# A two-layer expert network behind clustered attention: batch 1's tiles spaced wider, four tiles of batch 0 transposed on TensorE, sums of |v| on ScalarE

## The chip, the cores and the metric

One Trainium2 chip, one core of it. The metric is the device time in microseconds of one execution, lower is better; the median of three runs is given. TensorE is called PE in the rows, VectorE DVE, ScalarE ACT, GpSimd POOL and SyncE SP.

## The reference

Two batches of eight heads of attention with 768 queries and keys of width 64. A key is only seen by queries of the same cluster, where the cluster is the nearest of 16 centroids per head. The 1536 x 512 result then goes through two expert layers, each of two matrix products (512 to 2048 and back).

```
q_assign = argmax(q_n @ c_n.T); k_assign = argmax(k_n @ c_n.T)      # per head, normalised
scores = where(q_assign == k_assign, q @ k.T / 8, -1e9)
attn = softmax(scores); x = (attn @ v)  ->  [1536, 512]
h = x @ w_in;  g = max(h, 0) + alpha * min(h, 0);  x = g @ w_out       # layer 1
h = x @ w_in2; g = h * clip(h + 3, 0, 6) / 6;      out = g @ w_out2    # layer 2
```

Inputs and output are float32; the products are made of a high and a low part each, so that a product of two matrices is three passes on TensorE. The weights stand in memory as 64-bit values and are turned into float32 in the kernel.

## The kernel before

The kernel records operations and does not write them down in order: `op(engine, cost, fn, r, w, acq, vt, ...)` keeps an operation with what it reads and writes, the buffers it takes, an estimated cost and a due time `vt`. `Planner.plan` then walks through time: each engine that is free takes the ready operation with the smallest due time for which buffers are free, for as long as its cost says. The start times of that plan are the order in which the instructions are issued, on every engine's own in-order queue. So the numbers at the top (`U0`, `T1`, `DU`, `T2`, `PREP0`, `ST`, ...) and the costs set the order and nothing else.

*Attention* (`attention`) runs for batch 0 and then for batch 1, as four pairs of heads (`prep`) of twelve tiles each (`head`, 128 queries by 768 keys; 48 tiles a batch). `prep` transposes q and k of a pair on TensorE (L461), splits them into high and low parts, makes the logits of the clusters (L518) from `cs`, which GpSimd fills from the centroid blocks `ccol` (L505, L507), picks the cluster on VectorE (L531 to L566), and scales v by a power of two taken from the maximum of |v| (L590 to L627). A tile makes its scores on TensorE (L662, a PSUM buffer `ps`), their minimum on VectorE (L669), the exponential on ScalarE (L696 or L676), and a high and a low part of 16 bits (`hl`, L730 and L734, or L681 and L685). These are transposed by a DMA on SP's queue into `pt` (`turn`, L640), and 18 short matmuls with v end the tile (`pv`, L647). Some tiles of batch 0 (`t % 4 == 2`) are transposed on TensorE instead (L709), with the two parts made behind it (L714, L718). From `EARLY = 44` on, the last four tiles of batch 0 take the way of L676, L681, L685 and the DMA. The due time of tile u is `U0 * u` in batch 0 and `T1 + 5 + DU * u` in batch 1.

*The expert layers* (`moe`) follow for batch 0 with due times from T1 to T1 + T2, and at the same time the tiles of batch 1 are worked off; then for batch 1 alone. A product is 12 matmuls: of w_in (`g_in`, L894, then ScalarE L902 or L911, VectorE L906 or L915) or w_out (`g_out`, L943 in layer 1, L946 in layer 2). L915 belongs to layer 2 alone. For batch 0 each of the 64 weight tiles (`weight`) is loaded (L800, L803), converted on ScalarE (L809) and VectorE (L814, L821, L827), stored for batch 1 (L832), and split by ScalarE and GpSimd (L836, L841). For batch 1 it is loaded back (L792).

## Time and profile before

| | |
|---|---|
| median of 3 runs | 828.1 us (825.6 to 828.75) |
| profiled execution | 828.88 us |
| its span, first to last instruction | 826.8 us |
| busy: TensorE, VectorE, ScalarE, GpSimd | 752.8, 522.7, 472.1, 477.9 us |
| mean granted TensorE clock | 0.959 |

The profile is of one execution. Busy times are sums over the span and hide that the stretches differ: the attention of batch 0, batch 0's expert layers with the attention of batch 1, and batch 1's expert layers have different busiest engines.

### The profile page before, as it was taken

The page shows a single profiled execution, that of the slowest core. Times are in us where ns is not written, and L with a number is a line of the kernel's source. Part 1 is how long each engine was busy: PE and PEld are TensorE (multiplying, and loading weights), DVE is VectorE, ACT ScalarE, POOL GpSimd, SP SyncE. Part 2 cuts the span into 40 slices and gives each one's busy share as a digit, 9 for nine tenths or more (in the row PEclk, how much of TensorE's full clock was granted, in tenths as well). Part 3 has the DMA queues.
Part 4 walks back from the last instruction along what each step waited for, and adds up shares of the span by engine and source line. Part 5 has one row for each costly group of instructions (what it writes and reads, how often), then busy time and mean ns, then how long its engine had stood idle before and what let it go on. Part 6 is the DMA issues. An engine that isn't in the chain of part 4 may idle for free.

```text
span 826.8 us, 14279 instructions
## 1 busy us (share of the span) xinstructions
PE 752.8 (91%) x5331; PEld 696.7 (84%) x5331; DVE 522.7 (63%) x882; ACT 472.1 (57%) x768; POOL 477.9 (58%) x450
## 2 busy tenths in 40 slices
PE   5667877678999999989999999999999999999997
PEld 4556766668999888879899988789999999899986
DVE  7997888988879988988986788621122222122222
ACT  6777858766576676676666554544433254443421
POOL 3685685638553574654765565765566377464630
PEclk9988898859999999998999999999999999999999
DMA  6589989998699999599985564543222121221201
GB/s 131 119 170 227 176 151 198 168 238 210 182 209 201 203 221 229 117 222 208 213 226 187 177 191 156 191 117 111 64 77 64 45 84 52 64 76 53 76 10 68
DMA packets 214533, 121.56 MB, mean 147 GB/s; under 512 B 171072, under 2 KB 191552, under 8 KB 214464
## 3 DMA queue, kind: packets, MB, share of 16 engines
q1 hardware_dynamic: 214464, 120.66, 61.4%
q8 instruction: 41, 0.67, 0.4%
q14 instruction: 28, 0.23, 0.1%
HBM read 61.38 MB, written 21.50 MB: 100 GB/s over the span
## 4 chain that ended last, share of the span: by engine, by line
PE 58%; DVE 17%; DMA 10%; ACT 6%; issue 4%; POOL 3%; SPq 1%; POOLq 0%; ACTq 0%; DVEq 0%
PE pb L894 12%; PE pc L894 12%; PE pc L943 7%; PE pb L943 6%; PE pc L946 6%; PE pb L946 5%; DMA pt<-hl 4%; PE ps L662 4%; DVE wf L821 3%; DVE junk L669 3%; PE ps L518 3%; DVE wf L827 3%; DMA wd<-in_moe_w_in_dram 2%; DVE wf L814 1%; PE pb L647 1%
## 5 line engine op out<-in xcount | busy, mean ns | idle before, releaser
L841 POOL TENSOR_TENSOR w<-wf,w 128x512 fp32r<-128x512 f32 x128 | 167.5, 1312 | 171.1 <-ACT w L836 122.9
L924 POOL TENSOR_TENSOR big<-t,big 128x384 fp32r<-128x384 f32 x128 | 139.0, 1090 | 80.9 <-ACT big L920 74.3
L894 PE MATMUL pb<-xh,w 128*128 128x384 f32 x528 | 143.5, 338 | 1.7 <-DVE vs L613 1.7
L894 PE MATMUL pc<-xh,w 128*128 128x384 f32 x496 | 136.7, 341 | 0.0
L836 ACT CAST w<-wf 128x512 fp32r<-128x512 f32 x125 | 77.0, 618 | 83.7 <-DVE wf L827 37.7
L734 POOL TENSOR_TENSOR hl<-e,hl 128x768 f16<-128x768 f32 x53 | 90.3, 1711 | 47.4 <-ACT hl L730 38.6
L894 PEld LDWEIGHTS pb<-xh,w 128*128 128x128 f32 x528 | 96.5, 187 | 2.4 <-DVE vs L613 2.0
L669 DVE TENSOR_SCALAR_CACHE_REDUCE junk<-ps 128x768 bf16<-128x768 f32 x96 | 91.0, 948 | 10.4 <-PE ps L662 7.6
L894 PEld LDWEIGHTS pc<-xh,w 128*128 128x128 f32 x496 | 91.6, 189 | 0.2
L894 PE MATMUL pb<-xl,w 128*128 128x384 f32 x264 | 89.1, 338 | 0.0
L920 ACT CAST big<-t 128x384 fp32r<-128x384 f32 x124 | 63.2, 513 | 41.1 <-DVE t L915 20.0
L894 PE MATMUL pc<-xl,w 128*128 128x384 f32 x248 | 84.2, 340 | 0.0
L946 PE MATMUL pc<-w,big 128*128 128x512 f32 x312 | 77.0, 400 | 2.0 <-POOL big L924 1.9
L662 PE MATMUL ps<-big,big 128*128 128x384 f32 x192 | 59.6, 394 | 18.9 <-ACT e L696 6.2
L943 PE MATMUL pb<-big,w 128*128 128x384 f32 x396 | 75.8, 344 | 0.3 <-ACT t L999 0.3
L946 PEld LDWEIGHTS pc<-w,big 128*128 128x128 f32 x312 | 59.2, 192 | 16.2 <-POOL big L924 3.6
L943 PE MATMUL pc<-big,w 128*128 128x384 f32 x372 | 71.5, 342 | 0.0
L943 PEld LDWEIGHTS pb<-big,w 128*128 128x128 f32 x396 | 70.9, 190 | 0.6 <-ACT t L999 0.4
L696 ACT ACTIVATE e<-ps,mn 128x768 f32<-128x768 f32 x60 | 53.6, 902 | 23.6 <-DVE junk L669 22.1
L821 DVE SCALAR_TENSOR_TENSOR wf<-wd,wf 128x512 int32<-128x512 int32 x64 | 66.0, 1031 | 1.3
L943 PEld LDWEIGHTS pc<-big,w 128*128 128x128 f32 x372 | 66.3, 190 | 0.0
L946 PE MATMUL pb<-w,big 128*128 128x512 f32 x264 | 63.9, 393 | 2.0 <-POOL big L924 2.0
(144 smaller groups left out, 1335.5 us busy)
## 6 DMA issues: line engine op xcount, KB each, us to landing
wd<-in_moe_w_in_dram SPq DMA_DIRECT2D x32, 512.0 KB, 4.5
w<-wf SPq DMA_DIRECT2D x64, 256.0 KB, 3.2
wd<-in_moe_w_out_dram SPq DMA_DIRECT2D x32, 512.0 KB, 4.3
wf<-w SPq DMA_DIRECT2D x64, 256.0 KB, 2.6
raw_q<-in_q_dram SPq DMA_DIRECT2D x16, 192.0 KB, 3.7
raw_k<-in_k_dram SPq DMA_DIRECT2D x16, 192.0 KB, 3.8
raw_v<-in_v_dram SPq DMA_DIRECT2D x16, 192.0 KB, 3.3
out_dram<-acc SPq DMA_DIRECT2D x12, 256.0 KB, 2.0
```

Of the source, the lines that this page charges most:

```text
L662: nc.tensor.matmul(ps.ap[:, kk, 0:NH], s[x].ap[:, i, c0:c0 + 128], s[y].ap[:, kk, :], start=(n == 0), stop=(n == 1))
L669: nc.vector.tensor_scalar(out=junk.rearrange("p (a b) -> p a b", a=2), in0=ps.ap[:, :, 0:NH], scalar1=LN_P, scalar2=None, op0=ALU.add, op1 ...
L696: nc.scalar.activation(out=e.ap.rearrange("p (a b) -> p a b", a=2), in_=ps.ap[:, :, 0:NH], func=ACTF.Exp, bias=mn.ap, scale=-1.0)
L734: tt_on(eng)(out=hl.ap[:, 1, :], in0=e.ap, in1=hl.ap[:, 0, :], op=ALU.subtract)
L821: nc.vector.scalar_tensor_tensor(out=wi, in0=wd.ap[:, :, 1], scalar=-0x80000000, in1=wi, op0=ALU.bitwise_and, op1=ALU.bitwise_or)
L836: copy_on(e)(w.ap[:, 0, :], wf.ap)
L841: tt_on(e)(out=w.ap[:, 1, :], in0=wf.ap, in1=f32(w.ap[:, 0, :]), op=ALU.subtract)
L894: nc.tensor.matmul(hp.ap[:, 0:NH], w.ap[:, hw, 128 * kk:128 * kk + 128], (xl if hx else xh)[i][:, kk, :], start=(m == 0), stop=(m == 3 * K ...
L920: copy_on(e)(g.ap[:, 0, :], t.ap)
L924: tt_on(e)(out=g.ap[:, 1, :], in0=t.ap, in1=f32(g.ap[:, 0, :]), op=ALU.subtract)
L943: nc.tensor.matmul(o.ap[:, 0:NH], w.ap[:, hw, 128 * e:128 * e + 128], g.ap[:, hg, :], start=(m == 0), stop=(m == 3 * FC - 1))
L946: nc.tensor.matmul(o.ap, g.ap[:, hg, 128 * e:128 * e + 128], w.ap[:, hw, :], start=(m == 0), stop=(m == 3 * FC - 1))
```

## The change

The table of numbers at the top changes, and with it the order. Batch 1's tiles are due every 5.216 instead of every 3.672, so that they reach further into the expert layers of batch 0, which in turn are due within 313 instead of 329. Some twelve estimated costs change too. In the code, the last four tiles of batch 0 are transposed on TensorE (L709 before), as every fourth was. The scale of v is taken from the sum of |v| over each partition's 384 values times 2^-9, made by two ScalarE activations with an accumulator, and no longer from a maximum on VectorE. The centroid blocks `ccol` and the memset of `cs` go from VectorE to GpSimd. A one-column exponential is issued right behind the square root, so that its table is loaded there.

```diff
-U0, PREP0, SPAN0 = 2.2, -23.969, 15.768
-T1, DU, PREP1, SPAN1 = 110.562, 3.672, -22.219, 20.627
-T2, LEAD, LOADS = 329.488, 19.217, 14.435
-S_AT, PV_AT, LAZY = -0.999, -0.056, 0.0
+U0, PREP0, SPAN0 = 2.345, -16.443, 11.495
+T1, DU, PREP1, SPAN1 = 110.896, 5.216, -24.195, 27.638
+T2, LEAD, LOADS = 313.132, 24.352, 12.015
+S_AT, PV_AT, LAZY = -3.092, 1.619, 0.0
...
+        op("ACT", 1.5, lambda: nc.scalar.activation(out=first, in_=three, func=ACTF.Exp), r=["three"], w=["first"],
+           after=[o], vt=vt)
...
-            nc.vector.tensor_scalar(out=ccol[:, 0, :], in0=f32(hi), scalar1=-1.0, scalar2=None, op0=ALU.mult)
...
+            nc.gpsimd.tensor_scalar(out=ccol[:, 0, :], in0=f32(hi), scalar1=-1.0, scalar2=None, op0=ALU.mult)
...
-                nc.vector.tensor_reduce(out=va.ap[:, 0, :], in_=vr.ap, axis=AX.XY,
-                                        op=ALU.max, apply_absolute_value=True)
-            op("DVE", 0.87, f, r=[(vr, 0), (vr, 1)], w=[(va, 0)], acq=[va], vt=vt)
+                for j in range(2):
+                    nc.scalar.activation(out=junk2.rearrange("p (t d) -> p t d", t=NT), in_=vr.ap[:, j], func=ACTF.Abs,
+                                         scale=2.0 ** -9, accum_out=va.ap[:, 0, j:j + 1])
+            op("ACT", 1.1, f, r=[(vr, 0), (vr, 1)], w=[(va, 0)], acq=[va], vt=vt)
...
-                if late and (b == 0 or t % 3):
+                if b and t % 3:
...
-                if b == 0 and t % 4 == 2:
+                if b == 0 and (late or t % 4 == 2):
```

What the order does at two places. First VectorE's queue around the last tiles of batch 0, before (`wf` are weight tiles, `hl` low parts of tiles, `xl` the attention result's low part for the expert layers):

```order
L685 SCALAR_TENSOR_TENSOR hl_118<-ps_154,hl_118 128x768
L814 TENSOR_SCALAR wf_97<-wf_97 128x512
L602 TENSOR_REDUCE va_135<-pb_158 2x1
L603 TENSOR_SCALAR va_135<-va_135 2x1
L605 TENSOR_SCALAR va_135<-va_135 2x1
L607 TENSOR_SCALAR va_135<-ident,va_135 2x2
L993 SCALAR_TENSOR_TENSOR xl_74<-pb_157,xh_72 128x384
```

And after, where L727 is the low part behind a transpose on TensorE, L830 and L836 are the weights' (L821, L827 before), L1002 is L993 before, and L680 the minimum:

```order
L727 SCALAR_TENSOR_TENSOR acc_106<-ps_156,acc_106 128x768
L823 TENSOR_SCALAR wf_96<-wf_96 128x512
L830 SCALAR_TENSOR_TENSOR wf_96<-wd_94,wf_96 128x512
L727 SCALAR_TENSOR_TENSOR acc_105<-ps_157,acc_105 128x768
L836 SCALAR_TENSOR_TENSOR wf_96<-wd_94,wf_96 128x512
L823 TENSOR_SCALAR wf_97<-wf_97 128x512
L755 TENSOR_SCALAR sm_150<-pb_159,vs_135 128x6
L757 RECIPROCAL sm_150<-sm_150 128x6
L758 TENSOR_TENSOR xn_137<-pb_159,sm_150 128x6x64
L830 SCALAR_TENSOR_TENSOR wf_97<-wd_95,wf_97 128x512
L680 TENSOR_SCALAR junk,mn_141<-ps_155 128x768
L836 SCALAR_TENSOR_TENSOR wf_97<-wd_95,wf_97 128x512
L1002 SCALAR_TENSOR_TENSOR xl_74<-pb_159,xh_72 128x384
```

The first product's L906 is row 248 of VectorE's order before; after, it is row 231 (as L915 there). Next SP's queue in the second expert layer of batch 0, before (L803 and L800 load weights, L832 stores them, L1000 is the last pair's result of batch 1's attention):

```order
L832 DMA w_159<-wf_96 128x512
L1000 DMA xb<-t_101 128x384
L1000 DMA xb<-t_102 128x384
L803 DMA wd_94<-in_moe_w_out_dram 128x1024
L832 DMA w_159<-wf_97 128x512
L803 DMA wd_95<-in_moe_w_out_dram 128x1024
```

And after, likewise at two loads of w_out (L812 and L809 load, L841 stores, L651 is the transposing DMA of a tile):

```order
L841 DMA w_160<-wf_96 128x512
L812 DMA wd_94<-in_moe_w_out_dram 128x1024
L651 DMA_TRANSPOSE pt_109<-hl_118 128x12x128
L651 DMA_TRANSPOSE pt_108<-hl_119 128x12x128
L812 DMA wd_95<-in_moe_w_out_dram 128x1024
L841 DMA w_160<-wf_97 128x512
```

Before, the last pair of batch 1 is through when these loads stand there; after, its tiles still stand between loads.

## Rows read from the trace of the kernel before

**Rows 1.** The page: busy us of the engines (share of the span, instructions), and shares of the span in the chain that ended last, by engine.

```profile
PE 752.8 (91%) x5331; PEld 696.7 (84%) x5331; DVE 522.7 (63%) x882; ACT 472.1 (57%) x768; POOL 477.9 (58%) x450
...
PE 58%; DVE 17%; DMA 10%; ACT 6%; issue 4%; POOL 3%; SPq 1%; POOLq 0%; ACTq 0%; DVEq 0%
```

**Rows 2.** Single instructions in order of time on TensorE and VectorE: start and duration in us, engine, line, operation.

```profile
180.33 0.67 PE L894 MATMUL pc<-xh,w 128*128 128x384 f32 x1
...
395.41 0.34 PE L894 MATMUL pc<-xh,w 128*128 128x384 f32 x1
...
397.53 0.34 PE L894 MATMUL pb<-xh,w 128*128 128x384 f32 x1
...
401.52 0.69 DVE L827 SCALAR_TENSOR_TENSOR wf<-wd,wf 128x512 uint32<-128x512 uint32 x1
402.12 0.95 DVE L685 SCALAR_TENSOR_TENSOR hl<-ps,hl 128x768 f16<-128x768 f32 x1
...
403.94 0.54 DVE L915 SCALAR_TENSOR_TENSOR t<-t,pc 128x384 f32<-128x384 f32 x1
```

**Rows 3.** Pieces of the chain that ended last, in order of time: start and length in us, engine, tile, line, matmuls.

```profile
144.67 3.21 PE pb L647 x90
...
271.79 0.65 PE ps L461 x6
...
283.57 1.48 PE ps L662 x8
...
542.57 4.19 PE pc L894 x24
...
703.09 5.50 PE pb L946 x24
```

**Rows 4.** Busy time of each engine in four stretches: from and to, length in us, busy us (instructions) of PE, PE's weight loads, DVE, ACT, POOL, then the granted clock, the DMA engines' busy share and GB/s.

```profile
0.00:180.33 180.33, 127.81 (x1327) 109.19 (x1328) 153.66 (x300) 131.79 (x170) 109.70 (x130) 0.86 0.88 173
180.33:395.41 215.08, 202.84 (x1702) 193.68 (x1701) 189.54 (x315) 144.40 (x233) 121.86 (x109) 0.97 0.89 202
395.41:542.57 147.16, 143.65 (x830) 130.15 (x830) 113.70 (x159) 82.75 (x149) 92.29 (x75) 0.99 0.67 192
542.57:826.80 284.23, 278.55 (x1476) 263.67 (x1475) 65.75 (x110) 113.16 (x216) 154.02 (x138) 1.00 0.22 66
```

**Rows 5.** VectorE's groups of instructions by line: operation, tiles, shapes, count, busy us and mean ns of one, idle us ahead of them and who ended it.

```profile
L669 DVE TENSOR_SCALAR_CACHE_REDUCE junk<-ps 128x768 bf16<-128x768 f32 x96 | 91.0, 948 | 10.4 <-PE ps L662 7.6 <-DVE junk L669 0.5 <-PE pb L597 0.2
L821 DVE SCALAR_TENSOR_TENSOR wf<-wd,wf 128x512 int32<-128x512 int32 x64 | 66.0, 1031 | 1.3
L827 DVE SCALAR_TENSOR_TENSOR wf<-wd,wf 128x512 uint32<-128x512 uint32 x64 | 59.3, 927 | 0.8
L814 DVE TENSOR_SCALAR wf<-wf 128x512 int32<-128x512 int32 x64 | 41.9, 655 | 16.1 <-ACT wf L809 16.1
L685 DVE SCALAR_TENSOR_TENSOR hl<-ps,hl 128x768 f16<-128x768 f32 x36 | 34.1, 949 | 4.2 <-ACT hl L681 1.9 <-POOL v L627 1.4 <-DMA w<-wf 0.6
...
L491 DVE SCALAR_TENSOR_TENSOR kb<-ps,big 64x768 fp32r<-64x768 f32 x16 | 15.2, 953 | 0.4 <-ACT big L487 0.2
...
L543 DVE TENSOR_TENSOR eq<-lg,mx 128x384 bf16<-128x384 f32 x8 | 9.6, 1197 | 0.1
L531 DVE STREAM_TRANSPOSE lg<-ps 128x384 f32<-128x384 f32 x16 | 8.5, 562 | 7.4 <-PE ps L518 7.0 <-ACT kb L575 0.3
L566 DVE STREAM_TRANSPOSE lg<-oh 128x768 f32<-128x768 f32 x8 | 7.8, 971 | 3.8 <-POOL oh L561 3.8
L669 DVE DVE_READ_ACCUMULATOR junk<-ps 128x1 f32 x96 | 7.7, 80 | 0.0
L590 DVE TENSOR_REDUCE va<-raw_v 128x2 f32<-128x768 f32 x8 | 7.6, 952 | 0.6 <-DMA raw_v<-in_v_dram 0.3
...
L556 DVE TENSOR_TENSOR eq<-desc,mx 128x384 bf16<-128x384 bf16 x8 | 5.2, 650 | 0.1
...
L535 DVE TENSOR_REDUCE mx<-lg 128x24 f32<-128x384 f32 x8 | 4.3, 541 | 0.0
...
L718 DVE SCALAR_TENSOR_TENSOR acc<-ps,acc 128x768 f16<-128x768 f32 x4 | 3.8, 944 | 0.7 <-ACT acc L714 0.7
...
L358 DVE MEMSET cs<- 128x1024 f32 x1 | 0.9, 912 | 0.2 <-issue 0.2
...
L410 DVE CAST ccol<-chi 64x128 fp32r<-64x128 f32 x2 | 0.5, 236 | 0.0
```

**Rows 6.** The same columns as rows 4, for the stretch up to the first instruction of layer 2 on VectorE.

```profile
0.00:403.94 403.94, 337.93 (x3081) 309.65 (x3082) 351.60 (x627) 282.24 (x413) 237.27 (x243) 0.92 0.89 189
```

**Rows 7.** Two of ScalarE's groups by line, with the columns of rows 5.

```profile
L911 ACT ACTIVATE t<-pb,three 128x384 f32<-128x384 f32 x34 | 19.7, 579 | 22.5 <-PE pb L894 22.5
...
L990 ACT CAST xh<-pb 128x384 fp32r<-128x384 f32 x8 | 3.8, 477 | 3.8 <-PE pb L761 3.7
```

**Rows 8.** ScalarE's instructions around the first exponential, in order of time; in brackets the idle time ahead of one, and who ended it.

```profile
27.64 1.28 ACT L696 ACT_TABLE_LOAD   x1
29.13 0.90 ACT L696 ACTIVATE e<-ps,mn 128x768 f32<-128x768 f32 x1 [0.21 <-DVE junk L669]
```

**Rows 9.** DMA issues by line: queue, operation, count, median us from issue to landing.

```profile
pt<-hl SPq DMA_TRANSPOSE x69, 4.7
```

**Rows 10.** Waits of SP's queue: us in total, times, longest us; the first from 180.33 to 395.41 us, the second from 395.41 to 542.57.

```profile
SPq L640 <- DVE hl L685: 28.6, 13, 7.3
...
SPq L803 <- DVE wf L827: 20.9, 5, 4.7
```

More of the change, by code (lines that the diff above doesn't have):

```diff
@@ L313 @@
     junk = sb.tile([128, S], BF16, name="junk")
+    junk2 = sb.tile([128, NT * D], BF16, name="junk2")
     hls = slots(2, [128, 2, S], FP16, "hl")
@@ L346, in constants @@
         cn = sm.tile([128, 2, D], F32, name="cn")
+        first = sm.tile([128, 1], F32, name="first")
         hi = sm.tile([128, 128], F32R, name="chi")
@@ L357, in f @@
             nc.vector.memset(f32(ccol), 0.0)
-            nc.vector.memset(f32(cs), 0.0)
-        op("DVE", 2.0, f, w=["cs", "three", "ones", "ccol"], vt=vt)
+        op("DVE", 1.1, f, w=["three", "ones", "ccol"], vt=vt)
         def f():
@@ L370, in constants @@
         op("POOL", 3.6, f, w=["desc", "oh", "kb", "v1"], vt=vt)
+        op("POOL", 1.0, lambda: nc.gpsimd.memset(f32(cs), 0.0), w=["cs"], vt=20.0)
         def f():
@@ L383, in constants @@
         op("DVE", 0.4, f, r=["cr"], w=["ss"], vt=vt)
-        op("ACT", 0.1, lambda: nc.scalar.activation(out=ss[:, 1:2], in_=ss[:, 0:1], func=ACTF.Sqrt), w=["ss"], vt=vt)
+        o = op("ACT", 0.1, lambda: nc.scalar.activation(out=ss[:, 1:2], in_=ss[:, 0:1], func=ACTF.Sqrt), w=["ss"], vt=vt)
+        op("ACT", 1.5, lambda: nc.scalar.activation(out=first, in_=three, func=ACTF.Exp), r=["three"], w=["first"],
+           after=[o], vt=vt)
         def f():
@@ L404, in f @@
                                            op0=ALU.mult, op1=ALU.subtract)
-            nc.vector.tensor_scalar(out=ccol[:, 0, :], in0=f32(hi), scalar1=-1.0, scalar2=None, op0=ALU.mult)
-            nc.vector.tensor_scalar(out=ccol[:, 1, :], in0=f32(lo), scalar1=-1.0, scalar2=None, op0=ALU.mult)
+        op("DVE", 0.6, f, r=[pt], w=["chl"], vt=vt)
+        def f():
+            nc.gpsimd.tensor_scalar(out=ccol[:, 0, :], in0=f32(hi), scalar1=-1.0, scalar2=None, op0=ALU.mult)
+            nc.gpsimd.tensor_scalar(out=ccol[:, 1, :], in0=f32(lo), scalar1=-1.0, scalar2=None, op0=ALU.mult)
             for j in range(2):
                 a, z = slice(64 * j, 64 * j + 64), slice(64 - 64 * j, 128 - 64 * j)
-                nc.vector.tensor_copy(ccol[a, 2 + 2 * j, :], f32(hi)[a])
-                nc.vector.tensor_copy(ccol[z, 2 + 2 * j, :], f32(lo)[z])
-                nc.vector.tensor_copy(ccol[a, 3 + 2 * j, :], f32(hi)[a])
-        op("DVE", 1.6, f, r=[pt], w=["ccol"], vt=vt)
+                nc.gpsimd.tensor_copy(ccol[a, 2 + 2 * j, :], f32(hi)[a])
+                nc.gpsimd.tensor_copy(ccol[z, 2 + 2 * j, :], f32(lo)[z])
+                nc.gpsimd.tensor_copy(ccol[a, 3 + 2 * j, :], f32(hi)[a])
+        op("POOL", 2.0, f, r=["chl"], w=["ccol"], vt=vt)
         op("SP", 0.5, lambda: nc.sync.dma_start(out=alpha_sb, in_=moe_alpha.rearrange("(k p) -> p k", p=128)),
@@ L520, in prep @@
                               (("qa", "h"), ("qa", "l"), ("ka", "h"), ("ka", "h2"), ("kb", "l"))]
-                op("PE", 1.3, f, r=r + [(s["kb"], "m") for s in st], w=[(pl, i)],
+                op("PE", 1.42, f, r=r + [(s["kb"], "m") for s in st], w=[(pl, i)],
                    acq=[pl] if i == 0 else [], vt=vt, lat=0.3)
@@ L544, in f @@
                                         op=ALU.is_equal)
-            op("DVE", 0.8, f, r=[(lg, 0), (lg, 1), (mx, 0)], w=[(eq, 0)], acq=[eq], vt=vt, lat=0.13)
+            op("DVE", 1.2, f, r=[(lg, 0), (lg, 1), (mx, 0)], w=[(eq, 0)], acq=[eq], vt=vt, lat=0.13)
             def f():
@@ L566, in f @@
                 nc.vector.transpose(lg.ap.rearrange("p a b -> p (a b)"), oh.rearrange("p a b -> p (a b)"))
-            op("DVE", 0.87, f, r=["oh"], w=[(lg, 0), (lg, 1)], vt=vt)
+            op("DVE", 0.98, f, r=["oh"], w=[(lg, 0), (lg, 1)], vt=vt)
             vt = v0 + span * ST[4]
@@ L604, in f @@
                                         scalar2=None, op0=ALU.bitwise_and)
-                nc.vector.tensor_scalar(out=a[:, 1, 0:1], in0=a[:, 1, 0:1], scalar1=2.0 ** -96, scalar2=1.0 / V_SCALE,
+                nc.vector.tensor_scalar(out=a[:, 1, 0:1], in0=a[:, 1, 0:1], scalar1=2.0 ** -96, scalar2=2.0 ** 9 / V_SCALE,
                                         op0=ALU.max, op1=ALU.mult)
@@ L619, in f @@
                                             scalar2=None, op0=ALU.mult)
-            op("POOL", 1.3, f, r=[vs], w=[(vr, 0), (vr, 1)], vt=vt)
+            op("POOL", 2.5, f, r=[vs], w=[(vr, 0), (vr, 1)], vt=vt)
             def f(e):
@@ L730, in f @@
                     copy_on(eng)(hl.ap[:, 0, :], e.ap)
-                pick(("ACT", "DVE"), (0.84, 0.8), f, r=[e], w=[(hl, 0)], acq=[hl], vt=vt)
+                pick(("ACT", "DVE"), (0.84, 0.56), f, r=[e], w=[(hl, 0)], acq=[hl], vt=vt)
                 def f(eng, e=e, hl=hl):
@@ L750, in f @@
                                         in1=m.unsqueeze(2).to_broadcast([128, NT, D]), op=ALU.mult)
-            op("DVE", 1.06, f, r=[(o, t) for t in range(NT)] + [vs], w=[(xn, j), sm],
+            op("DVE", 0.97, f, r=[(o, t) for t in range(NT)] + [vs], w=[(xn, j), sm],
                acq=[sm] + ([xn] if j == 0 else []), vt=vt)
@@ L907, in fn @@
                                                in1=hp.ap[:, 0:NH], op0=ALU.mult, op1=ALU.add)
-            op("DVE", 0.58, fn, r=[hp, "alpha"], w=[t], vt=vt)
+            op("DVE", 0.61, fn, r=[hp, "alpha"], w=[t], vt=vt)
         else:
```

20 lines of the change are left out of this document (9 added, 11 removed).

## The prediction

> **What bounds the kernel now.** I read the busy times first. TensorE is the busiest engine, with 752.8 us of 826.8 [rows 1], but that is an average over stretches with different limits, so I cut the span at three places that can be found in the order of the program as well as in the trace: the first matmul of the first expert layer (180.33), the first product of the second layer for batch 0 (395.41; its result reaches VectorE at 403.94) [rows 2], and the first product of batch 1's expert layers (542.57) [rows 3]. Call the four stretches A, B, C and D. The busy times of each stretch [rows 4] say this. In A, VectorE works 153.66 of 180.33 us, and no other engine comes near; TensorE waits, at a granted clock of 0.86. In B, VectorE (189.54 of 215.08) and TensorE are both nearly full. In C, VectorE falls to 113.70 of 147.16, and in D to 65.75 of 284.23, and TensorE goes from product to product without a gap, 24 matmuls in 4.19 us [rows 3].
>
> How much TensorE has to spare follows from counting. Matmuls of 384 columns at 0.177 us (the 12 of one product start at 395.41, those of the next at 397.53 [rows 2]), those of 512 columns at 0.229 (5.50 us for 24), the 18 of one attention tile's last product at 0.64 (90 in 3.21) and transposes at 0.11 (six in 0.65) [rows 3] make 195.2 us of work in B, 141.2 in C and 277.7 in D. So TensorE loses 19.9 us in B (10.2%), 6.0 in C (4.2%) and some 6 with the tail in D. **Until the second layer starts, VectorE sets the pace; after it, TensorE does.** That is the frame for the rest.
>
> **The change, part by part.** D holds the same instructions before and after, so its 284 us stay. I count what stands before the first instruction of the second layer on VectorE (L915 before, where it starts at 403.94): 535 instructions before, 492 after. The counts are from the two orders (beside a few of their rows above), the durations from [rows 5].
>
> - Batch 1 is spaced wider (DU from 3.672 to 5.216): 13 of its tiles' minima move behind that point, 13 x (0.948 + 0.080) = -13.4 us. Of the low-part subtractions 12 fewer stand there (eight belong to moved tiles), 12 x 0.949 = -11.4.
> - The last four tiles of batch 0 go over TensorE's transposes: four of the 12 subtractions come back as L718, 4 x 0.944 = +3.8. Four transposing DMAs go.
> - The maximum of |v| leaves VectorE (for a sum on ScalarE): 8 x 0.952 = -7.6.
> - One pair's cluster choice (2 x 0.562, 0.541 twice, 1.197, 0.650, 0.971) and its two subtractions of 0.953 move behind the point: -6.9 (the second 0.541 is taken for a like reduction).
> - The constants: a memset of 0.912 and eight block copies of at most 0.236 go to GpSimd, -2.7.
> - One weight more is prepared earlier, 0.655 + 1.031 + 0.927 = +2.6; some 20 short instructions that move both ways come to +2.5.
>
> Sum: -33.1 us of 384.9 (all 535 by their means). The records overlap: the instruction at 401.52 lasts 0.69, and the next starts at 402.12 [rows 2]. So the 384.9 are 351.60 us of busy VectorE [rows 6], a factor of 0.913, and 403.94 - 351.60 = 52.3 us are idle. If the idle time stays, A and B together lose 33.1 x 0.913 = 30.2 us; if it shrinks with the work, 403.94 x 33.1 / 384.9 = 34.7. I take -32.5, the middle, since the idle time is partly waits for the tiles that are moved (L669 for L662) and partly start-up, which stays.
>
> What was moved is paid for in C, on TensorE, which sets the pace there. By the order, C gains 15 tiles' scores of four matmuls (4 x 0.177 = 0.71 a tile; two follow each other in 1.48 [rows 3]: 10.6), 13 last products (8.3), the logits of one pair (2.8), and 12 transposes (1.4): 141.2 becomes 164.3, +23.1. At C's present loss of 4.2% that is +24.1; at B's loss of 10.2% C would take 181.0, +33.9. B's losses come where VectorE has more to do than TensorE. C before is 77% VectorE, and after, with 25 us more of it in some 172, about 81%; B is 88%. So I stay near the low end, **+25**. The net is -7.5 us.
>
> Edits that I cost at nothing, and what hides them:
>
> - The sums of |v| on ScalarE. No row shows such an instruction. Plain copies of 128x384 take 0.477, a rectification with a bias column 0.579 [rows 7]; reading out an accumulator costs VectorE 0.080. So each lies between 0.48 and 0.66, all 16 between 7.7 and 10.6; I take 0.55, near the copies (8.8). ScalarE is busy 131.79 of 180.33 us in A and 144.40 of 215.08 in B [rows 4]; if the cover failed, the price is those 8.8 less the 7.6.
> - The exponential's table early. It is loaded at 27.64 for 1.28 us, and the first exponential starts at 29.13 after 0.21 us of waiting for VectorE's minimum [rows 8]. So the load is hidden already: gain 0. The Trainium skill, "ScalarE: Activation LUTs", What ACT_TABLE_LOAD costs, puts a switch at about 2.66 us with its drain; by that figure the sum would be -10.2 instead of -7.5. This trace shows the 1.28 and no drain on the path.
> - The centroid blocks on GpSimd: eight copies of about 0.2 and the memset. The logits that read them wait for the operands from ScalarE and VectorE too, so I take 0; if they were late, about 2 us at the start.
>
> Against the sums of |v|: one reduction is 0.952 on VectorE, and two passes on ScalarE are 0.96 to 1.32, so the work itself gets no cheaper; what speaks for the move is who has room in A and B. The Trainium skill, "ScalarE: Activation LUTs", Rules for kernel authors, sends relu, max and the like to VectorE rather than ScalarE; by that rule the sums would stay, and VectorE's relief would be -25.5 in place of -33.1.
>
> **The rivals.**
>
> *The relief is not on the path (about no change).* If A and B give only 25 of the 32.5, C takes it all. For it: the chain of waits is DMA for 10% and ScalarE for 6% [rows 1], and the DMA engines are 0.88 to 0.89 busy in A and B [rows 4], so a tile's transposing DMA, 4.7 us from issue to landing [rows 9], may pace what VectorE does not. Against it: the same tiles take their DMAs with them, and the four transposes on TensorE remove four more. Time: 828, give or take 2.
>
> *TensorE takes over in B too (more gain).* B after holds 174.9 us of TensorE work. At C's loss of 4.2% it would last 182.2, 32.9 less; with 12 us from A and +25 in C the net is -20: 808. The 12 us of A: the instructions ahead of VectorE's first product result (L906) fall from 168.1 to 155.6 us by their means, 12.5 x 0.913. For it: B before loses its 19.9 us where VectorE is behind. Against it: VectorE's work in B only falls in step (216.8 to 196.2 by the means, 179 after the factor), so it is still the longer of the two there.
>
> *Slower: the weights come late in C.* SP's queue is in order, and some 12 transposing DMAs more now stand between the weight loads of C (13 more tiles end there; seven did before). In B, SP waited 28.6 us in 13 waits for the tile's low part (L640 for L685) [rows 10], 2.2 each, with weight loads queued behind. In C before, SP already waits 20.9 us for VectorE at loads of w_out (L803) [rows 10]. Twelve waits of 2.2 us are 26 us of delay on SP; if half reaches TensorE through ScalarE's L809, VectorE and GpSimd, C loses 13 us more: 833.6. It decides from 7.5 us on. Against it: in the order, VectorE's finished weights (L827) stand three to five ahead of TensorE's need at nearly every fourth product, as before; and a tile of batch 1 has, between its scores and its last product, 11 to 22 us of other TensorE work where it had 9 to 17 from the first product on, against some 8.3 us for the tile's own steps: 0.95 for the minimum, 0.90 for the exponential [rows 8], some 0.8 for a copy (like [rows 7], over twice the columns), 0.95 for the low part, 4.7 for the DMA.
>
> **How the numbers follow.** The profiled execution took 828.88 us, 0.8 above the median of 828.1 of the runs shown. Against that median: 828.1 - 7.5 = 820.6, so **821 us**. What a measurement of this kernel can tell from no change is about 0.5%, 4.1 us, so faster means under 824. I give the forecast 0.53, the relief off the path 0.19, TensorE everywhere 0.14, late weights 0.14. The ends of the forecast's own terms (-34.7 + 24.1 and -30.2 + 33.9, the last unlikely) are 817.5 and 831.8; its own range is 815 to 825. For 8 in 10, I go from 810, which leaves out half of the largest gain, to 831, which leaves out most of the late weights. Faster: nearly all of the forecast and the larger gain, 0.63; slower 0.16; the same 0.21.
>
> **What would show it.** In the changed kernel the first expert matmul comes at about 168 (it is 180.33), the second layer's first product on TensorE at 363 (395.41), the first of batch 1 at 535 (542.57), and D stays at 284. VectorE's busy time up to the second layer is near 321. The table load shows no effect: the first exponential stays near 29. If A and B shrink by less than 25, the relief was not on the path, and VectorE's idle time will have grown past 52 us. If C is longer than 181, weights or transposes are late, and TensorE's waits for GpSimd's w or for pt, and SP's waits ahead of the loads, will say which. I would be wrong most simply if ScalarE, with 16 passes more, became what the tiles wait for in A.

## The result: 806.3 us, a ratio of 0.973

The changed kernel takes 806.28 us in the median (804.28 to 807.28, four runs) where the kernel before takes 828.42 (825.6 to 831.27, four runs): a ratio of 0.973, 95% interval 0.9691 to 0.9768. The forecast was 821 with a range from 810 to 831, so the sign was right and the gain is more than twice the forecast. The profiled execution took 805.96 us.

The page of the changed kernel, with the rows that answer to [rows 1] (busy us of the engines; shares of the chain that ended last):

```profile
PE 743.6 (92%) x5355; PEld 688.8 (86%) x5355; DVE 515.0 (64%) x873; ACT 475.1 (59%) x793; POOL 484.0 (60%) x459
...
PE 64%; DVE 17%; issue 5%; POOL 5%; ACT 4%; DMA 4%; SPq 0%; POOLq 0%; DVEq 0%; ACTq 0%
```

DMA fell from 10% of the chain to 4%, TensorE rose from 58% to 64%, and VectorE's 17% did not move. The four stretches of the changed kernel, cut at the same places and with the columns of [rows 4]:

```profile
0.00:164.31 164.31, 122.25 (x1315) 106.05 (x1316) 140.76 (x273) 123.29 (x175) 111.39 (x138) 0.93 0.86 165
...
164.31:355.04 190.73, 180.04 (x1417) 171.55 (x1416) 170.44 (x277) 131.39 (x220) 117.93 (x104) 0.99 0.88 210
355.04:523.58 168.54, 166.35 (x1151) 151.10 (x1151) 138.01 (x215) 107.52 (x183) 100.58 (x81) 0.99 0.78 200
523.58:804.20 280.62, 274.98 (x1477) 260.13 (x1476) 65.76 (x110) 112.94 (x216) 154.14 (x138) 1.00 0.23 68
```

Against [rows 4], A is 16.0 us shorter, B 24.4 shorter, C 21.4 longer and D 3.6 shorter. So B and C nearly cancel here, and the result is A's 16 us, 3 us of B and C together, and 3.6 of D, in which no instruction changed.

Both kernels were run side by side once more. The table has these two and all the experiments below: the four stretches of the profiled execution, cut at the 1st, 385th and 769th matmul with w_in (L894 before; the first row is cut as in [rows 4], and by the 769th matmul its C is 147.0 and its D 284.4); the time at which VectorE starts its first instruction of layer two; and the device time, with its ratio to the kernel before on the same chip. The stretches are those of one execution, the median that of n. In e6 and e15 the profiled execution, with 826.05 and 816.27 us, is some 4 us longer than the median.

| kernel | A | B | C | D | VectorE at layer two | median us (n) | ratio, 95% |
|---|---|---|---|---|---|---|---|
| before (first profile) | 180.3 | 215.1 | 147.2 | 284.2 | 403.9 | 828.42 (4) | 1 |
| after (first profile) | 164.3 | 190.7 | 168.5 | 280.6 | 370.0 | 806.28 (4) | 0.973, 0.969-0.977 |
| c_before | 180.9 | 211.3 | 147.9 | 284.4 | 400.7 | 826.31 (1) | |
| c_after | 164.8 | 191.4 | 168.5 | 284.3 | 371.2 | 810.74 (1) | |
| e1_order_alone | 172.9 | 181.9 | 171.7 | 280.3 | 364.0 | 809.65 (4) | 0.979, 0.975-0.983 |
| e2_edits_alone | 172.4 | 219.0 | 148.4 | 281.7 | 398.0 | 822.7 (10) | 0.997, 0.994-1.000 |
| e3_max_on_dve | 169.0 | 190.4 | 168.4 | 284.3 | 374.3 | 814.2 (4) | 0.982, 0.977-0.987 |
| e4_consts_table_back | 163.9 | 190.2 | 168.5 | 284.3 | 369.0 | 808.45 (4) | 0.977, 0.974-0.979 |
| e5_last_four_old | 171.4 | 195.1 | 171.6 | 284.5 | 370.1 | 824.09 (10) | 0.996, 0.994-0.998 |
| e6_du_3672 | 164.9 | 218.4 | 156.6 | 284.4 | 396.8 | 821.9 (10) | 0.994, 0.992-0.997 |
| e8_du_525 | 164.1 | 190.7 | 172.0 | 280.2 | 381.6 | 809.58 (4) | 0.982, 0.977-0.988 |
| e9_min_twice | 166.0 | 197.2 | 171.1 | 280.6 | 377.9 | 817.25 (4) | 0.990, 0.985-0.994 |
| e10_scores_more | 165.8 | 194.8 | 171.8 | 281.9 | 375.3 | 816.24 (4) | 0.989, 0.985-0.993 |
| e11_last_four_dma_kept | 172.6 | 189.8 | 167.0 | 283.0 | 377.4 | 814.61 (4) | 0.986, 0.982-0.990 |
| e12_last_four_dma | 174.8 | 190.6 | 168.3 | 281.8 | 380.3 | 816.96 (5) | 0.989, 0.985-0.994 |
| e13_du_alone | 184.4 | 185.3 | 168.7 | 281.8 | 391.3 | 821.77 (10) | 0.996, 0.993-0.999 |
| e14_tiles_later_6 | 164.5 | 190.7 | 169.8 | 283.7 | 360.3 | 811.69 (4) | 0.984, 0.981-0.988 |
| e15_tiles_later_15 | 166.1 | 198.1 | 165.8 | 284.5 | 371.6 | 812.28 (4) | 0.986, 0.982-0.990 |

### The profile page after: what moved, and what is told of

It reads as the page before. It is cut to its first block, busy times and chain, and to the rows that moved or that the text cites. A ratio compares the mean times of both kernels' runs of the same rounds, so it can differ in the third digit from the quotient of the medians.

```text
span 804.2 us, 14356 instructions
## 1 busy us (share of the span) xinstructions
PE 743.6 (92%) x5355; PEld 688.8 (86%) x5355; DVE 515.0 (64%) x873; ACT 475.1 (59%) x793; POOL 484.0 (60%) x459
## 4 chain that ended last, share of the span: by engine, by line
PE 64%; DVE 17%; issue 5%; POOL 5%; ACT 4%; DMA 4%; SPq 0%; POOLq 0%; DVEq 0%; ACTq 0%
PE pc L903 15%; PE pb L903 14%; PE pb L955 9%; PE pc L955 7%; PE pb L952 6%; PE pc L952 5%; DVE junk L680 3%; PE ps L673 3%; DVE wf L830 2%; DMA wd<-in_moe_w_in_dram 2%; DVE wf L823 2%; DVE wf L836 2%; POOL hl L743 2%; PE ps L526 1%; POOL raw_v L629 1%
## 5 line engine op out<-in xcount | busy, mean ns | idle before, releaser
L933 POOL TENSOR_TENSOR big<-t,big 128x384 fp32r<-128x384 f32 x128 | 137.1, 1074 | 89.9 <-ACT big L929 77.4
L903 PE MATMUL pc<-xh,w 128*128 128x384 f32 x520 | 144.8, 340 | 0.0
L680 DVE TENSOR_SCALAR_CACHE_REDUCE junk<-ps 128x768 bf16<-128x768 f32 x96 | 91.0, 948 | 9.0 <-PE ps L673 4.5
L903 PEld LDWEIGHTS pc<-xh,w 128*128 128x128 f32 x520 | 96.1, 190 | 0.4
L903 PEld LDWEIGHTS pb<-xh,w 128*128 128x128 f32 x504 | 92.1, 188 | 0.2
L952 PE MATMUL pb<-big,w 128*128 128x384 f32 x444 | 83.6, 338 | 0.7 <-DVE xn L758 0.5
L952 PEld LDWEIGHTS pb<-big,w 128*128 128x128 f32 x444 | 77.3, 188 | 1.7 <-DVE xn L758 0.8
L955 PE MATMUL pb<-w,big 128*128 128x512 f32 x312 | 76.8, 393 | 2.0 <-POOL big L933 2.0
L955 PEld LDWEIGHTS pb<-w,big 128*128 128x128 f32 x312 | 58.1, 188 | 14.9 <-POOL big L933 3.1
L955 PE MATMUL pc<-w,big 128*128 128x512 f32 x264 | 64.4, 393 | 0.3 <-POOL big L933 0.3
L830 DVE SCALAR_TENSOR_TENSOR wf<-wd,wf 128x512 int32<-128x512 int32 x64 | 62.6, 978 | 1.0
L952 PE MATMUL pc<-big,w 128*128 128x384 f32 x324 | 61.2, 337 | 1.6 <-POOL w L850 1.6
L955 PEld LDWEIGHTS pc<-w,big 128*128 128x128 f32 x264 | 49.3, 188 | 10.9 <-POOL big L933 0.7
```

Of the source, the lines that this page charges most:

```text
L680: nc.vector.tensor_scalar(out=junk.rearrange("p (a b) -> p a b", a=2), in0=ps.ap[:, :, 0:NH], scalar1=LN_P, scalar2=None, op0=ALU.add, op1 ...
L830: nc.vector.scalar_tensor_tensor(out=wi, in0=wd.ap[:, :, 1], scalar=-0x80000000, in1=wi, op0=ALU.bitwise_and, op1=ALU.bitwise_or)
L903: nc.tensor.matmul(hp.ap[:, 0:NH], w.ap[:, hw, 128 * kk:128 * kk + 128], (xl if hx else xh)[i][:, kk, :], start=(m == 0), stop=(m == 3 * K ...
L933: tt_on(e)(out=g.ap[:, 1, :], in0=t.ap, in1=f32(g.ap[:, 0, :]), op=ALU.subtract)
L952: nc.tensor.matmul(o.ap[:, 0:NH], w.ap[:, hw, 128 * e:128 * e + 128], g.ap[:, hg, :], start=(m == 0), stop=(m == 3 * FC - 1))
L955: nc.tensor.matmul(o.ap, g.ap[:, hg, 128 * e:128 * e + 128], w.ap[:, hw, :], start=(m == 0), stop=(m == 3 * FC - 1))
```

## The experiments

Three theories are told apart. **One**, the prediction's: VectorE paces all that comes ahead of layer two, TensorE what follows. **Two**: in B, too, TensorE's own work sets the pace, and VectorE counts in A alone. **Three**: in B each engine waits for the other in turn, and a microsecond of either is worth a part of itself. Line numbers are those of the kernel that is spoken of.

**The two kernels again.** 

> The kernel before, unchanged, profiled beside the changed one on one chip. In the two profiles so far the last stretch (batch 1's expert layers, the same instructions in both) lasts 284.2 us before and 280.5 after, since a product there takes 2.12 us before and 2.08 after. If that difference is of the chip or the run, both kernels show the same product time here, and the last stretch is equal within 1 us. If the change makes TensorE's products shorter, it is 284 here and 280 in the changed one again.

> The changed kernel, unchanged, on the same chip as the one before. Of the 22.6 us between the two profiles, 3.8 lie in the last stretch; if they are the chip's, the two spans differ by about 19 here, if they are the change's, by about 23.

Side by side, A is 16.1 us shorter, B 19.9 shorter, C 20.6 longer and D the same: -15.5 in all. The 3.6 us of D in the first pair belong to that execution and not to the change, and side by side the gain is 15.5 us where the medians above give 22. The chain in D, the first profile of the changed kernel:

```profile
602.50 2.08 PE pb L952 x12
```

and the same kernel in its second profile (c_after), at the same granted clock of 1.00:

```profile
602.66 2.12 PE pc L952 x12
```

Twelve matmuls take 2.08 us in one execution and 2.12 in the other.

**The order alone and the edits alone.** e1 is the kernel before with all of the change's numbers (the table at the top, and the fifteen costs that the planner gives its operations). e2 is the changed kernel with the old ones. Of e1's diff, the table and two of the costs:

```
-U0, PREP0, SPAN0 = 2.2, -23.969, 15.768
-T1, DU, PREP1, SPAN1 = 110.562, 3.672, -22.219, 20.627
-T2, LEAD, LOADS = 329.488, 19.217, 14.435
+U0, PREP0, SPAN0 = 2.345, -16.443, 11.495
+T1, DU, PREP1, SPAN1 = 110.896, 5.216, -24.195, 27.638
+T2, LEAD, LOADS = 313.132, 24.352, 12.015
...
-                    o_p = op("PE", 1.2, f, r=["ident", e], w=[pe], acq=[pe, pt], vt=vt, lat=0.3)
+                    o_p = op("PE", 0.72, f, r=["ident", e], w=[pe], acq=[pe, pt], vt=vt, lat=0.3)
...
-                pick(("ACT", "DVE"), (0.84, 0.8), f, r=[e], w=[(hl, 0)], acq=[hl], vt=vt)
+                pick(("ACT", "DVE"), (0.84, 0.56), f, r=[e], w=[(hl, 0)], acq=[hl], vt=vt)
```

> The kernel before with the new table of numbers and the new costs alone; the |v| maximum, the constants and the last four tiles of batch 0 stay as they were. VectorE has 354.0 us of counted work up to layer two (351.8 in the changed kernel, 384.9 before), and 164.0 up to the first product (155.6, 168.1). Theory one, VectorE's work up to layer two sets the time: about 2 us slower than the changed kernel, 808. Theory two, the order has little part in it and the edits are what removes the waits: 820 or more.

> The changed code with the old table of numbers and old costs. VectorE has 377.8 us of counted work up to layer two, 7.1 less than before, and TensorE's work in the third stretch is that of before (141.2). Theory one, VectorE's work: 6.5 us faster than before, 822. Theory two, the edits carry the gain: 812 or less.

The numbers give 2.1%, the edits by themselves 0.3% (0 to 0.6). Each shortens A by 7 to 9 us; only the numbers move work from B to C. Both times are near those of theory one (808 and 822). In e1, A, B and C together take 526.5 us, in the changed kernel 523.6 and 524.7, before 542.4 and 540.1: e1's A is 8 to 9 us longer than in the changed kernel, but its B, in an order of its own, is 9 to 10 shorter. So the numbers alone carry most of the gain, and A's 16 us are not the only way to it.

**The spacing of batch 1.** e6 takes the spacing back in the changed kernel:

```
-T1, DU, PREP1, SPAN1 = 110.896, 5.216, -24.195, 27.638
+T1, DU, PREP1, SPAN1 = 110.896, 3.672, -24.195, 27.638
```

e13 changes it alone in the kernel before:

```
-T1, DU, PREP1, SPAN1 = 110.562, 3.672, -22.219, 20.627
+T1, DU, PREP1, SPAN1 = 110.562, 5.216, -22.219, 20.627
```

> The changed kernel with the old spacing of batch 1's tiles (DU 3.672) and all else as changed. VectorE has 374.6 us of counted work up to layer two, 22.8 more than the changed kernel; TensorE 150.0 in the third stretch, 14.3 less. Theory one: the second layer starts 21 to 28 us later, the third stretch is 14 to 15 shorter, the time 7 to 13 us longer than the changed kernel's. If the second and third stretch together depend on TensorE's work and a fixed loss alone, the spacing gives nothing: within 3 us.

> The kernel before with one number changed, the spacing of batch 1 (5.216 for 3.672). Counted from the order: TensorE in B 195.2 to 174.8 us, in C 141.2 to 161.6; VectorE ahead of the second layer 384.9 to 373.8, ahead of the first product's result unchanged. Theory one (VectorE paces B): B -10, C +20: 837 us. Theory two (TensorE's own work sets both): B -20, C +20: 826, no change; then the whole gain of the change lies in A. Theory three (a microsecond of either engine in B is worth about 0.4, and in C one of TensorE 0.8 to 1): B -13, C +16 to +20: 830 to 834. If instead it gains 15 us or more, the spacing alone carries the result.

Without the wider spacing, A keeps its 164.9 us, B grows by 27 and C falls by 12: it costs 13 to 15, where theory one wanted 7 to 13. Alone it shortens B by 26 to 30, lengthens C by 21, A is 3.5 to 4 longer, and the kernel gains 0.4% (0.1 to 0.7). So the spacing moves work from B to C as the prediction said, in both directions, but is not the gain by itself. e13 misses all three theories: they wanted 10, 20 and 13 us less in B, and B lost 26 to 30. Why the spacing is worth 13 to 15 us in the one kernel and 4 in the other shows in part in TensorE's waits. In B of e6 (us in total, times, longest):

```profile
PE pc L952 <- DVE t L915: 3.1, 1, 3.1
...
PE pc L903 <- DVE t L915: 2.4, 1, 2.4
PE pb L903 <- DVE t L915: 1.6, 1, 1.6
```

and in B of the changed kernel:

```profile
PE pb L952 <- DVE t L915: 0.2, 1, 0.2
```

With the tiles close together, VectorE comes 7.1 us late with the first layer's results (L915), which in the changed kernel hardly happens.

**The maximum of |v|, the constants and the table.** Both kernels keep the order of the change. e3 takes the maximum back to VectorE:

```
-                for j in range(2):
-                    nc.scalar.activation(out=junk2.rearrange("p (t d) -> p t d", t=NT), in_=vr.ap[:, j], func=ACTF.Abs,
-                                         scale=2.0 ** -9, accum_out=va.ap[:, 0, j:j + 1])
+                nc.vector.tensor_reduce(out=va.ap[:, 0, :], in_=vr.ap, axis=AX.XY,
+                                        op=ALU.max, apply_absolute_value=True)
```

e4 takes the memset and the centroid blocks back to VectorE and drops the early exponential (one of the eight blocks is shown):

```
-        op("POOL", 1.0, lambda: nc.gpsimd.memset(f32(cs), 0.0), w=["cs"], vt=20.0)
+        op("POOL", 1.0, lambda: nc.vector.memset(f32(cs), 0.0), w=["cs"], vt=20.0)
...
-        op("ACT", 1.5, lambda: nc.scalar.activation(out=first, in_=three, func=ACTF.Exp), r=["three"], w=["first"],
+        op("ACT", 1.5, lambda: None, r=["three"], w=["first"],
...
-            nc.gpsimd.tensor_scalar(out=ccol[:, 0, :], in0=f32(hi), scalar1=-1.0, scalar2=None, op0=ALU.mult)
+            nc.vector.tensor_scalar(out=ccol[:, 0, :], in0=f32(hi), scalar1=-1.0, scalar2=None, op0=ALU.mult)
```

> The changed kernel in its own order, where the maximum of |v| alone is taken on VectorE again, at the place in the order where ScalarE has the two passes. That is 8 x 0.952 = 7.6 us more on VectorE up to layer two. Theory one, VectorE sets the pace up to layer two: the second layer's first product comes 7 to 9 us later, and the time is 7 to 9 us longer than the changed kernel's. Theory two, TensorE's work behind the first product plus a fixed loss sets the time, and only the first stretch counts: five of the eight maxima lie in the first stretch, so it grows by 5 and the rest not at all. Theory three, the place has slack: within 2 us of the changed kernel.

> The changed kernel in its own order, with the centroid blocks and the memset on VectorE again and without the early exponential. The forecast put 0 on both; by VectorE's count it is 2.7 us more there at the start, so 0 to 3 us slower than the changed kernel. If the table load with its drain were on the path, the first exponential would come 1.3 to 2.7 us later than its place in the changed kernel.

e3: A is 4.2 us longer than in c_after, B and C are the same. Five of the eight maxima stand in A, 5 x 0.952 = 4.8 us: in A, VectorE's work is worth nearly its full length; the three in B cost nothing. This is theory two's outcome (5 in A, nothing behind it) and not theory one's 7 to 9. e4 changes no stretch by more than 1.3 us against c_after. The table load, in ScalarE's order of time, the changed kernel:

```profile
3.19 1.28 ACT L388 ACT_TABLE_LOAD   x1
...
30.57 0.90 ACT L705 ACTIVATE e<-ps,mn 128x768 f32<-128x768 f32 x1 [2.00 <-DVE junk L680]
```

and e4:

```profile
29.50 1.28 ACT L705 ACT_TABLE_LOAD   x1
31.50 0.90 ACT L705 ACTIVATE e<-ps,mn 128x768 f32<-128x768 f32 x1 [0.72 <-DVE junk L680]
```

The first exponential does come 0.93 us earlier, and waits for VectorE's minimum in both; A ends at 164.3 and 163.9.

**The last four tiles of batch 0.** Before, seven of batch 0's 48 tiles (one in six) were transposed on TensorE. e5 takes back the edit for the last four and lets the planner make its order anew:

```
-                if b and t % 3:
+                if late and (b == 0 or t % 3):
...
-                if b == 0 and (late or t % 4 == 2):
+                if b == 0 and t % 4 == 2:
```

e11 and e12 keep the order, and replace for these tiles alone the transposes by the DMA; ScalarE's copy then reads the exponential itself (e12 shown, where hx is one of the two hl buffers):

```
-                        for x in range(NT):
+                        for x in range(0 if late else NT):
...
+                        if late:
+                            nc.scalar.copy(hx[:, 0, :], e.ap)
+                            nc.vector.tensor_tensor(out=hx[:, 1, :], in0=e.ap, in1=hx[:, 0, :], op=ALU.subtract)
+                            return
...
+                        if late:
+                            nc.sync.dma_start_transpose(out=pt.ap, in_=hx.rearrange("p a s -> p (a s)"))
+                            return
```

In e11 the subtraction stands beside the DMA, behind the next tile's exponential, which writes the same buffer: three of these tiles get their low part from the wrong tile. In e12 it stands ahead of it.

> The changed kernel with the last four tiles of batch 0 by the DMA again (the planner makes a new order of it). VectorE has 342.3 us of counted work up to layer two, 9.5 less than the changed kernel. Theory one, VectorE's count: 5 to 9 us faster than the changed kernel up to layer two. If the transposes on TensorE are what shortens the first stretch (the wait of the last tiles for their DMA at the half clock before): the first stretch is 4 to 8 us longer, 168 to 172 in place of 164, and the time is longer by part of that.

> The changed kernel, its order kept, where only the last four tiles of batch 0 go back to a transposing DMA: no transposes on TensorE, ScalarE's copy and VectorE's low part read the exponential itself (the same number of instructions on each), and SP issues the four DMAs. Theory one (VectorE's count sets A; the prediction costed this edit by its VectorE work alone): no change, 806 to 810 us. Theory two (the first expert layer waits for these last tiles, so their 4.7 us from issue to landing, queued one behind the other on SP among weight loads, stand on the path): A grows by 5 to 10 us, B stays or gives 2 back, C and D stay: 812 to 818.

> As the run before with the last four tiles of batch 0 back on transposing DMAs and the order kept, but VectorE's low part now stands before the next tile's exponential, which writes the same buffer (in that earlier run it read the next tile's exponential, so its output differed from the reference). Theory one (VectorE's count sets A): 806 to 810 us, A 164. Theory two (the first expert layer waits for the last tiles' DMAs): A 171 to 174, B and C as in the changed kernel, 813 to 816 us, as in that earlier run.

In e12, B and C are those of the changed kernel, and A is 10 to 10.5 us longer, with VectorE busy no more than in the changed kernel (columns of [rows 4]):

```profile
0.00:174.77 174.77, 127.06 (x1291) 110.10 (x1292) 139.56 (x273) 123.56 (x175) 111.51 (x138) 0.85 0.87 164
```

TensorE's last products of these tiles, in a stretch from 140 to 185 us (busy us, mean ns, then the idle time ahead of them and who ended it), in the changed kernel:

```profile
L658 PE MATMUL pb<-v,acc 128*128 128x65 f16 x144 | 5.2, 193 | 0.0
```

and in e12:

```profile
L658 PE MATMUL pb<-v,acc 128*128 128x65 f16 x144 | 6.2, 206 | 9.9 <-DMA acc<-hl 9.9
```

The 9.9 us are TensorE standing before the landing of these DMAs, with the first expert layer queued behind. While it stands, the granted clock falls as well, to 0.50, the lower of its two levels (1.2 GHz); over all of A it is 0.85 where the changed kernel has 0.93:

```profile
155.00:165.00 10.00, 2.01 (x34) 1.68 (x31) 6.06 (x10) 6.51 (x12) 2.71 (x3) 0.50 0.98 179
```

A part of e12's price is the edit's own: the four tiles share one buffer for the exponential, so in e12 the next exponential also waits for the subtraction. e11, where it does not, has the same wait (9.7 us) and an A that is 7.8 to 8.3 us longer. So VectorE's count alone (theory one) does not set A.

The same DMAs did not cost this much in the kernel before. There, in the stretch from 140 to 185 us:

```profile
L647 PE MATMUL pb<-v,acc 128*128 128x65 f16 x144 | 6.7, 213 | 2.8 <-DMA acc<-hl 2.8
```

What stood beside them shows when A is cut once more, at the scores of the last tile ahead of these four. Up to there the two kernels take 138.3 and 137.1 us, with VectorE busy for 114.78 and 115.28. The rest of A, before and after:

```profile
138.34:180.33 41.99, 29.87 (x310) 24.94 (x311) 38.88 (x68) 29.49 (x41) 18.91 (x22) 0.67 0.94 195
```

```profile
137.08:164.31 27.23, 21.94 (x303) 20.17 (x304) 25.48 (x52) 18.74 (x30) 17.10 (x21) 0.94 0.82 161
```

So 14.8 of A's 16.0 us are gained in its tail, where VectorE has 13.4 us less to do and is 93% busy before and 94% after. Before, that tail held six subtractions of the preparation of pairs of heads (four L491, two L476) and the conversions of four weights; after, it has none of the former and the conversions of two weights. The granted clock in it rises from 0.67 to 0.94; what that is worth by itself no run separates.

e5 misses both of its forecasts in time: A is 7 us longer, as its second theory said, but so are B by about 4 and C by 3, and the time is 13 to 18 us longer. TensorE's wait for these DMAs is only 1.2 us there, so e5's longer A has other causes than e12's.

**VectorE's arrival at layer two.** Three changed kernels with a number a little off. TensorE's counted work differs by at most 0.7 us in B and C; VectorE's work ahead of layer two differs by +12.3, -9.9 and -6.6. First e8, then e14 (e15 has 20.0 in place of 11.0):

```
-T1, DU, PREP1, SPAN1 = 110.896, 5.216, -24.195, 27.638
+T1, DU, PREP1, SPAN1 = 110.896, 5.25, -24.195, 27.638
```

```
-        attention(1, lambda u: T1 + 5.0 + DU * u,
+        attention(1, lambda u: T1 + 11.0 + DU * u,
```

> The changed kernel with one number of its table a little off: the spacing of batch 1 is 5.25 in place of 5.216. TensorE has the same work in each stretch (174.9 us counted in B, 164.3 in C), but the order comes out differently for VectorE: 364.1 us counted ahead of its first instruction of the second layer, where the changed kernel has 351.8. Theory one (VectorE paces everything ahead of the second layer, as the prediction had it): A and B together grow by 12.3 x 0.913 = 11 us, C and D stay: 818 us against 807 to 809. Theory two (TensorE's own work sets B and C, VectorE counts in A alone): A has the same VectorE count, so no change, 806 to 810. A third outcome, a difference that neither count explains, would be the size of the noise that a re-planned order brings with it.

> The changed kernel with batch 1's tiles due 6 us later, all else the same: TensorE has the same work in each stretch to 0.7 us, VectorE as much ahead of the first product's result (155.6 us) but 341.9 ahead of the second layer, 9.9 less. Theory one (VectorE paces B): -9: 797 to 800 us. Theory two (TensorE's own work sets B): 806 to 810, with VectorE's first instruction of the second layer some 9 us earlier and TensorE's start there where it is. Theory three: -4: 803 to 805.

> The changed kernel with batch 1's tiles due 15 us later: one of its tiles leaves A (VectorE 152.4 us counted there for 155.6, TensorE four matmuls less), VectorE 345.2 ahead of the second layer for 351.8. If VectorE's count sets A one to one: A -3, and with theory two for B 803 to 806 us; with theory one for B 798 to 801. If A is set by batch 0's last tiles alone: 806 to 810.

The start of layer two on TensorE and on VectorE in e8:

```profile
354.78 0.34 PE L903 MATMUL pc<-xh,w 128*128 128x384 f32 x1
...
381.62 0.54 DVE L924 SCALAR_TENSOR_TENSOR t<-t,pc 128x384 f32<-128x384 f32 x1
```

and in e14:

```profile
355.23 0.34 PE L903 MATMUL pb<-xh,w 128*128 128x384 f32 x1
...
360.33 0.55 DVE L924 SCALAR_TENSOR_TENSOR t<-t,pb 128x384 f32<-128x384 f32 x1
```

VectorE arrives 11.6 us later in the one and 9.7 earlier in the other than the first profile's 370.0, as its count says. TensorE starts at 355 in all three, and e14, for which theory one wanted 797 to 800 us, takes 811.69, above every forecast. So VectorE's arrival there is a place in its queue and does not set TensorE's start. These runs do not say that VectorE's work in B is free: what they moved lies behind TensorE's start, and VectorE is busy in B for 172.4 and 171.7 us, as in the changed kernel (170.4). e15, meant also to empty A, misses every theory: A does not shrink, and in its profile B is 7 us longer than in e14. By the medians the two differ by only 0.6 us (812.28 and 811.69), so this belongs at least in part to that execution. None of the three beats the change.

**The price of an engine's work in B.** The order of the change is kept. e9 takes the minimum twice, e10 puts four more matmuls ahead of the scores, both for 24 tiles of batch 1. First e9, then e10:

```
+                    for _ in range(2 if b and j == 0 else 1):
+                        nc.vector.tensor_scalar(out=junk.rearrange("p (a b) -> p a b", a=2), in0=ps.ap[:, :, 0:NH],
+                                                scalar1=LN_P, scalar2=None, op0=ALU.add, op1=ALU.min, accum_out=mn.ap)
```

```
+                    for kk in range(2 if b and j == 0 else 0):
+                        for _ in range(2):
+                            nc.tensor.matmul(ps.ap[:, kk, 0:NH], s["qa"].ap[:, i, c0:c0 + 128], s["ka"].ap[:, kk, :],
+                                             start=True, stop=True)
```

> The changed kernel, its order kept, where VectorE takes the minimum of a tile's scores twice in 24 of batch 1's 48 tiles (same result). At 0.948 + 0.080 us each this is 3 more in A (+3.1), 15 in B (+15.4) and 6 in C (+6.2). Theory one (VectorE paces A and B): A and B together +17 to +18.5, C 0: 824 to 827 us. Theory two (TensorE's own work sets B): A +3, B and C 0 to +2: 810 to 813. Theory three (in B the two engines wait for each other in turn, so that work of either is worth a part of itself): about half, +9 in all: 817.

> The changed kernel, its order kept, with four more matmuls of 384 columns ahead of the scores of 24 of batch 1's tiles (their results are written over): 4 x 0.177 = 0.71 us of TensorE a tile, 3 tiles in A (+2.1), 15 in B (+10.6), 6 in C (+4.2). Theory one (TensorE has room in B, sets the pace in C): B 0 to +2, C +4.2: 811 to 814 us. Theory two (TensorE's own work sets B and C): B +10.6, C +4.2, A 0: 822. Theory three (each engine's work is worth a part of itself in B): B +5, C +4: 817.

B of e9 and of e10, with the columns of [rows 4]:

```profile
166.00:363.24 197.24, 183.16 (x1416) 173.72 (x1415) 186.39 (x310) 130.81 (x219) 115.96 (x104) 0.98 0.83 204
```

```profile
165.80:360.60 194.80, 188.11 (x1477) 180.73 (x1476) 169.89 (x278) 131.43 (x220) 116.55 (x104) 1.00 0.86 204
```

15.4 us more of VectorE lengthen B by 6.5 (0.42 of them), 10.6 us more of TensorE lengthen it by 4.1 (0.39); against c_after instead of the first profile it is 0.38 and 0.32. In C it is 2.5 of 6.2 for VectorE and 3.2 of 4.2 for TensorE. For work added to a kept order theory three holds in B: neither engine sets the pace alone. It does not carry over to a new order. By these prices B should have grown by 15 us in e6 (22.8 of VectorE, 14.3 of TensorE) and lost 13 in e13 (11.1 and 20.4), and it grew by 27 and lost 26 to 30.

## Why the prediction was right in sign and short by more than half

**A: -12 forecast, -16 measured.** The step that failed is the costing of the last four tiles, by their VectorE work alone (+3.8 for the L718, and four low parts less), with "four transposing DMAs go" at no price: in the changed order these DMAs cost 8 to 10.5 us (e11, e12), with VectorE's work the same. That A still came out within 4 us of the forecast is luck in part. The forecast took VectorE's relief to reach the path in full, and that holds only because the edit removed a wait that it had not counted. VectorE's busy time in A fell by 12.9 us (14.8 in the second pair), where the count gave 12.5 x 0.913 = 11.4, rounded up to 12; the rest is idle time of VectorE. This and the tail that VectorE fills before and after speak for the prediction's frame in A; that nothing else was gained there, such as the clock, is not shown. The sums of |v| are worth 4.2 (e3), as VectorE's count says, while in e9 3.1 us more of VectorE in A cost 1.2 to 1.7. The parts do not add up (7.4 for the numbers alone, 7.9 for the edits alone, but 10.5 + 4.2 for two edits in the new order).

**B: -20.5 forecast, -24.4 measured (-19.9 in the second pair).** The size was about right, the reason not. The step "VectorE's arrival at L915, so TensorE's start there" failed: VectorE arrived 34.0 us earlier (forecast -32.5; busy to there 325.6, forecast near 321, with 7.9 us less idle), while TensorE's start came 40.4 earlier, at 355.04 where I had 363. TensorE now runs 14.9 us ahead of VectorE there where it ran 8.5, and e8 and e14 show that this lead is free to change. The frame also stood against its own rows: in B, TensorE's counted 195.2 us are more than VectorE's 189.54 [rows 4], and the 216.8 us that were to make VectorE the longer of the two run up to its arrival at L915, past B's end. At the prices of e9 and e10, B should have lost 0.42 x 20.6 of VectorE and 0.39 x 20.3 of TensorE, together 16.6 us; the rest is order that I cannot break down. The rival "TensorE takes over in B" gave the time nearest to the result, 808, by luck: its -32.9 for B was 8 to 13 us too much, and its terms for A and C, the forecast's own, made up for it with 8 the other way.

**C: +25 forecast, +21.4 measured (+20.6).** The counted +23.1 of TensorE's work was paid at 0.93 of its length (in e10 at 0.77). The term that was mis-sized is the loss of 4.2% that I had added to it, and then rounded up. The late weights did not come: C is 168.5, well below the 181 that would have shown them.

**D: 0 forecast.** Right for the change; the 3.6 us are the rate of the first profiled execution.

In the first pair three terms were off by 3.6 to 4 us each, all to the same side, and D's rate added to them: -7.5 became -22.6. In the second pair A and C were off by 4 and B by less than 1, and it was -15.5.

**Edits at nothing.** The constants and the table cost and give nothing (e4), as forecast. The first exponential was to stay near 29 us and came at 30.57. The sums of |v| on ScalarE, whose price no row of before showed, are here (ns minimum, median, maximum):

```profile
L601 ACT ACTIVATE junk<-raw_v x16: 519/524/557, 14.2 to 288.0; 128x384 bf16<-128x384 f32 x16
L601 ACT ACTIVATION_READ_ACCUMULATOR junk<-raw_v x16: 185/187/222, 14.6 to 288.4; 128x1 f32 x16
```

0.524 us and 0.187 for reading out, partly on top of each other: 0.71 at most, a little above my bounds of 0.48 to 0.66. ScalarE's 16 passes cost up to 11.4 us and VectorE's eight 7.6, and the move still pays, since in A ScalarE has room (busy 123.29 of 164.31 us) and VectorE has little (140.76). By the rule of the Trainium skill that the prediction weighed ("ScalarE: Activation LUTs", Rules for kernel authors) the maximum would have stayed on VectorE; e3 does that and is 4.2 us longer in A, so here the measurement decides against it.

Left open: what sets B's length from one order to another, since the prices of e9 and e10 give about half of what e6 and e13 show; what the clock is worth in A's tail; and why taking back the four tiles' edit costs more with a new plan than in the kept order (e5, 822.6 us of span against 815.5 for e12).
